# Block transposes into contiguous scratch with ScalarE reordering, and expert weight loads kept in program order, in a sparse-attention and expert-layer kernel

## The chip, the cores and the metric

The kernel runs on one core of a Trainium2 chip. Its metric is the device time of one execution in microseconds (us). Three runs of the kernel before took 335.82, 336.32 and 337.53 us; the median is 336.32 us. The engines are TensorE (PE, with its weight loads PEld), VectorE (DVE), ScalarE (ACT), GpSimd (POOL) and SyncE (SP), which here only issues DMAs.

## The reference

Attention over 4 batches of 8 heads, 768 positions, head dimension 64, followed by a layer of 8 experts to which every token is assigned once, each expert taking exactly 384 of the 3072 tokens:

```python
def _attn_ref(q, k, v, n_global, n_local):          # n_global 8, n_local 96
    scores = scale * np.matmul(q, k.transpose(0, 1, 3, 2))
    keep = is_global | is_local                      # first 8 keys, or the last 96 up to the query
    scores = np.where(keep, scores + bias[None], -1e9)   # bias: -slope(head) * distance
    a = np.exp(scores - np.max(scores, axis=-1, keepdims=True))
    a = a / (np.sum(a, axis=-1, keepdims=True) + 1e-09)
    return np.matmul(a, v)

def _moe_ref(x, w_gate, w1, w2):                     # x: (3072, 512), 8 experts, F 1024
    logits = x @ w_gate
    # tokens in order of falling logit take their expert while it has room (384 each)
    for e in range(E):
        h = np.maximum(x[assigned == e] @ w1[e], 0.0)
        out[assigned == e] = h @ w2[e]
```

## The kernel before

The program has three stages, one after the other: attention, routing, experts.

**Attention** runs over 8 units u; a unit is half a batch, four heads. Its order is written out by hand in the loop at L460, and every engine follows it. For a unit, q and k arrive as 128 x 24 x 64 tiles (`kr`, `qr`: partition = head and block of 24 positions). VectorE transposes 32 x 32 blocks of them (`blocks`, L265): two calls for k (`kT`), two for q (`qT`), each 128 x 768 elements, and it writes the result in natural order, that is with neighbouring elements 24 positions (96 bytes) apart. ScalarE then copies k into seven overlapping tiles of 8 + 120 keys (`kA_out`, L273). `scores` (L307) multiplies in three groups, `expo` (L321) exponentiates each group on ScalarE, `mask` (L328, L335) multiplies by the mask on VectorE.

While unit u does this, unit u-1, whose two head pairs are A and B, is finished: `av` (L355) multiplies by v, `oT_out` (L360, ScalarE) takes the product out of PSUM, `sums` (L386, L389) forms row sums and gate logits in the PSUM tile `pr`, `sums_out` takes them out on VectorE, beginning with the transpose `LT` (L399), and `tok` (L419) transposes the heads on TensorE into `pk`, which VectorE scales (L427). `pr` and `pk` share two PSUM buffers, so the second `tok` of A waits until `LT` has emptied `pr`. The keys and queries of unit u+1 are transposed in between: `kT` at the start of the unit, `qT(0)` before `LT` of A, `qT(1)` behind it. There is one `kr` and one `qr` buffer; the load of unit u+2 is issued by SP after the transposes of u+1.

**Routing** (L566 to L851) is a chain of small VectorE and TensorE steps, which ends with the row numbers `idi`.

**Experts** (L853): `gather` (L866) fetches the 384 tokens of an expert in three indirect DMAs issued by GpSimd, `load_x` transposes them (L878, L879), then follow 32 matmuls with w1 (L897), the relu (L900), 24 matmuls with w2 (L906), the copy (L909) and three indirect scatters (L910). The weights of experts 0 and 1 are loaded during attention. The twelve late ones (w1 and w2 of experts 2 to 7, `late_weights`, L548) go into memory that attention used, so they are issued by GpSimd after it. They, the gathers and the scatters are all DMAs of GpSimd's one queue (q0). In the text four calls of `late_weights` stand ahead of routing and two in each expert's pass, around `gather(e + 2)`; outside the hand-ordered stretches a scheduler may move them.

Of the kernel before, what the change touches and what calls it, by code (L numbers as in the profile page):

```python
# [9 lines left out]
FP32 = mybir.dt.float32  # L10
# [20 lines left out]
KT = 120  # L31
NT = 7
# [10 lines left out]
def kernel(  # L43
# [159 lines left out]
    with ExitStack() as actx:  # L203
# [21 lines left out]
                                channel_multiplier=-1)  # L225
        natp = actx.enter_context(tc.tile_pool(name="natp", bufs=1))
        ktp = actx.enter_context(tc.tile_pool(name="ktp", bufs=2))
        tp = actx.enter_context(tc.tile_pool(name="tp", bufs=3))
        ppa = actx.enter_context(tc.tile_pool(name="ppa", bufs=4))
        ppb = actx.enter_context(tc.tile_pool(name="ppb", bufs=5))  # L230
# [8 lines left out]
        NJ = S_ // 32  # L239
        qr = natp.tile([128, NJ, D_], FP32)  # L240
        kr = natp.tile([128, NJ, D_], FP32)
        kTn = natp.tile([128, 2, NT * KT], FP32)
        v7s = [natp.tile([128, 2, NT, D_], FP32, name=f"v7_{i}") for i in range(NB)]
        kAs = {}
        qTs = {}
        LASTK = S_ - KT * (NT - 1)

        def load_u(u, dst, src):
# [13 lines left out]
            nc.sync.dma_start(v7[8 : 8 + LASTK, :, NT - 1, :],  # L262
                              v[b, h : h + 2, KT * (NT - 1) : S_].rearrange("t u d -> u t d"))

        def blocks(dst, src, g):  # L265
            nc.vector.transpose(out=dst[:, g, 0:S_].rearrange("p (c j) -> p j c", j=NJ),  # L266
                                in_=src[:, :, 32 * g : 32 * g + 32])

        def kT(u):
            for g in range(2):  # L270
                blocks(kTn, kr, g)

        def kA_out(u):  # L273
            kA = ktp.tile([128, 2, NT, 128], FP32, tag="kA", name=f"kA{u}")
            kAs[u] = kA
            nc.scalar.copy(out=kA[:, :, :, 8:128], in_=kTn.rearrange("p g (i k) -> p g i k", i=NT))
            nc.scalar.copy(out=kA[:, :, :, 0:8],  # L277
                           in_=kTn[:, :, 0:8].rearrange("p g (o k) -> p g o k", o=1).to_broadcast([128, 2, NT, 8]))

        def qT(u, g):  # L280
            if g == 0:
                qTs[u] = ktp.tile([128, 2, S_], FP32, tag="qT", name=f"qT{u}")
            blocks(qTs[u], qr, g)

        wpieces = []
        for e in range(W_EARLY):
# [10 lines left out]
                nc.gpsimd.dma_start(dst, s_)  # L297

        def scores(u, g):
            kA, qTt = kAs[u], qTs[u]  # L300
# [141 lines left out]
        with tc.manual_schedule():  # L442
            load_u(0, kr, k)
            load_u(0, qr, q)
            nc.vector.memset(kTn[:, :, S_:], 0.0)
            for i in range(NB):
                nc.vector.memset(v7s[i][:, :, NT - 1, :], 0.0)
            kT(0)
            load_u(1, kr, k)
            qT(0, 0)  # L450
            qT(0, 1)
# [4 lines left out]
            kA_out(0)  # L456
            for t in range(2):
                nc.gpsimd.tensor_scalar(out=wgx[64 * t : 64 * t + 64, :, 8 * t : 8 * t + 8],
                                        in0=wg_sb[64 * t : 64 * t + 64], scalar1=LSCALE, scalar2=None, op0=ALU.mult)
            for u in range(NU + 1):  # L460
                A, Bp = 2 * (u - 1), 2 * (u - 1) + 1
                cur, prev, nxt = u < NU, u > 0, u + 1 < NU
                if cur:
                    ps = scores(u, 0)
                    expo(u, 0, ps)
                    if u == 0:
                        for h in range(4):
                            build_W(h)
                if nxt:
                    kT(u + 1)  # L470
                    if u + 2 < NU:
                        load_u(u + 2, kr, k)
                if cur:
                    mask(2 * u, 0)
                    mask(2 * u + 1, 0)
# [7 lines left out]
                if nxt:  # L483
                    qT(u + 1, 0)
                    kA_out(u + 1)
                if prev:
                    sums_out(A, pr)
                weight_piece()
                if cur:
                    ps = scores(u, 1)  # L490
                    expo(u, 1, ps)
                    if u == 0:
                        for h in range(4, 8):
                            build_W(h)
                if nxt:
                    qT(u + 1, 1)
                    if u + 2 < NU:
                        load_u(u + 2, qr, q)
                if cur:
                    mask(2 * u, 1)  # L500
                    mask(2 * u + 1, 1)
                if prev and cur:
                    for hf in range(2):
                        pk = tok(A, hf)
                        tok_out(A, hf, pk)
                if prev:
                    av(Bp)
                    oT_out(Bp, 0)
# [36 lines left out]
    def late_weights():  # L545
        if lates:
            dst, s_ = lates.pop(0)
            nc.gpsimd.dma_start(dst, s_)  # L548

    for _ in range(4):  # L550
        late_weights()
# [301 lines left out]
    def experts(first):  # L853
        with ExitStack() as fctx:
# [7 lines left out]
            def gather(e):  # L862
                for t in range(TSLAB):
                    s = TSLAB * e + t
                    xe = gp.tile([128, DM], BF16, tag="xe", name=f"xe_{s}")
                    nc.gpsimd.indirect_dma_start(  # L866
                        out=xe, out_offset=None, in_=x_tok[:, :],
                        in_offset=bass.IndirectOffsetOnAxis(ap=idi[:, s : s + 1], axis=0),
                    )
                    xes[s] = xe  # L870

            def load_x(e):
# [87 lines left out]
```

## Time and profile before

| | |
|---|---|
| profiled execution | 337.55 us |
| its span, first to last instruction | 335.7 us |
| mean granted TensorE clock | 0.933 of full |
| attention, up to the first late weight | 178.8 us |
| routing, to the first gather | 32.2 us |
| first gather to the first expert matmul | 21.3 us |
| experts, to the end of the span | 103.4 us |
| busy: PE, DVE, ACT, POOL | 268.1, 188.0, 108.3, 80.7 us |

A mean over the whole span says little here, since the three stages have different limits: VectorE is nearly always busy in attention and little later. So the stretches are read one by one. An engine follows its own order; where it stands idle, the trace gives the length and what released it in square brackets. The 1.85 us between the profiled execution's time and its span lie outside the instructions.

### The profile page before, as it was taken

Reading aid. Unit: us, or ns where it says so; the run is one execution under the profiler, and the core shown is the slowest. Engines: PE = TensorE matmul, PEld = TensorE weight load, DVE = VectorE, ACT = ScalarE, POOL = GpSimd, SP = SyncE. Lnnn points to the kernel's source line nnn. Section 1 sums busy time; section 2 is a strip of 40 time slices with the busy share of each in tenths; the row PEclk is TensorE's granted clock in tenths of the full one; section 3 lists DMA queues with packets and bytes.
Section 4 is the critical chain, followed back from the end, with each engine's and each line's share of the span. In section 5 each row is a group of like instructions: output and inputs, shape, how many; then the busy total and the mean of one; then the engine's idle time right before and its main releaser. Section 6 shows DMA issues by size and latency. Waiting matters only on the chain. (4 is left out here: it accounts for less than half of the span.)

```text
span 335.7 us, 7401 instructions
## 1 busy us (share of the span) xinstructions
PE 268.1 (80%) x3174; PEld 182.4 (54%) x3174; DVE 188.0 (56%) x300; ACT 108.3 (32%) x177; POOL 80.7 (24%) x126
## 2 busy tenths in 40 slices
PE   0479559896998979899997889505999989999950
PEld 0367448685876858688874443103555545555520
DVE  4984597999998897996724667102121421332220
ACT  1395044545352443634310010000442233234400
POOL 4050000002077000000006100524664644311330
PEclk9999959999997989999996999955999999999995
DMA  4599565658979965422025999996799333111220
GB/s 187 183 191 202 193 169 144 173 146 195 208 120 266 238 161 146 99 52 51 2 49 85 211 209 210 211 209 197 126 212 288 109 111 127 62 61 66 96 96 6
DMA packets 52569, 49.27 MB, mean 147 GB/s; under 512 B 29745, under 2 KB 44081, under 8 KB 52529
## 3 DMA queue, kind: packets, MB, share of 16 engines
q0 software_dynamic: 15680, 26.22, 37.5%
q1 hardware_dynamic: 36848, 22.50, 25.6%
q8 instruction: 27, 0.44, 0.6%
q14 instruction: 14, 0.11, 0.1%
HBM read 56.05 MB, written 9.44 MB: 195 GB/s over the span
## 5 line engine op out<-in xcount | busy, mean ns | idle before, releaser
L307 PE MATMUL ps<-qT,kA 32*128 32x215 f32 (+2 forms) x896 | 52.3, 368 | 15.4 <-DVE qT L266 11.4
L900 ACT ACTIVATE hT<-ph 128x384 bf16<-128x384 f32 x64 | 30.9, 490 | 87.0 <-PE ph L897 51.1
L307 PEld LDWEIGHTS ps<-qT,kA 32*128 32x128 f32 x896 | 43.7, 207 | 21.9 <-ACT kA L277 11.4
L321 ACT ACTIVATE P<-ps 128x860 f32<-128x860 f32 (+1 forms) x48 | 40.8, 887 | 39.6 <-PE ps L307 38.4
L355 PE MATMUL po<-P,v 128*64 128x215 f32 (+6 forms) x576 | 44.7, 312 | 0.0
L355 PEld LDWEIGHTS po<-P,v 128*64 128x64 f32 x576 | 37.4, 148 | 9.2 <-issue 3.4
L335 DVE TENSOR_TENSOR P<-P,Wm 128x860 f32<-128x860 f32 (+1 forms) x32 | 33.2, 1056 | 12.2 <-ACT P L321 11.0
L266 DVE STREAM_TRANSPOSE kTn<-kr 128x768 f32<-128x768 f32 x16 | 31.9, 2098 | 12.5 <-DMA kr<-in_k_dram 12.5
L879 DVE COPY xT<-pxe 128x512 bf16<-128x512 bf16 x24 | 9.5, 421 | 48.6 <-PE pxe L878 32.8
L909 DVE COPY ot<-po 128x512 f32<-128x512 f32 x24 | 16.6, 691 | 33.8 <-PE po L906 26.1
L866 POOL DMA_INDIRECT xe<-x_tok,idi x24 | 23.3, 972 | 46.2 <-DVE idi L720 21.3
L897 PE MATMUL ph<-xT,w_late 128*128 128x384 bf16 x192 | 32.7, 326 | 1.4 <-ACT hT L900 1.0
L419 PE MATMUL pk<-ident,oT 128*128 128x128 f32 x96 | 17.6, 295 | 19.9 <-DVE LT L399 18.3
L910 POOL DMA_INDIRECT out_dram<-ot,idi x24 | 23.5, 978 | 40.6 <-DVE ot L909 37.4
L906 PE MATMUL po<-w_late,hT 128*128 128x512 bf16 x144 | 32.9, 379 | 0.0
L266 DVE STREAM_TRANSPOSE qT<-qr 128x768 f32<-128x768 f32 x16 | 32.9, 2080 | 0.0
L906 PEld LDWEIGHTS <-hT 128*128 128x128 bf16 x192 | 18.2, 98 | 19.5
L548 POOL DMA_DIRECT2D w_late<-in_moe_w_dram x12 | 10.1, 865 | 74.6 <-DVE x L427 71.1
L386 PE MATMUL pr<-P,onesx 128*32 128x192 f32 (+11 forms) x768 | 27.6, 259 | 0.0
L897 PEld LDWEIGHTS <-w_late 128*128 128x128 bf16 x192 | 18.8, 98 | 14.9 <-issue 2.1
L360 ACT COPY oT<-po 128x384 f32<-128x384 f32 x32 | 15.4, 480 | 34.6 <-PE po L355 34.6
L386 PEld LDWEIGHTS pr<-P,onesx 128*32 128x32 f32 x768 | 24.6, 109 | 2.2
(137 smaller groups left out, 248.2 us busy)
## 6 DMA issues: line engine op xcount, KB each, us to landing
w_late<-in_moe_w_dram POOLq DMA_DIRECT2D x12, 1024.0 KB
kr<-in_k_dram SPq DMA_DIRECT2D x8, 768.0 KB
qr<-in_q_dram SPq DMA_DIRECT2D x8, 768.0 KB
v<-in_v_dram SPq DMA_DIRECT2D x32, 180.0 KB
w_early<-in_moe_w_dram POOLq DMA_DIRECT2D x8, 512.0 KB
x_tok<-x SPq DMA_DIRECT2D x32, 96.0 KB
v<-in_v_dram SPq DMA_DIRECT2D x32, 14.0 KB
v<-in_v_dram SPq DMA_DIRECT2D x16, 24.0 KB
```

Source lines behind the costliest of these rows:

```text
L266: nc.vector.transpose(out=dst[:, g, 0:S_].rearrange("p (c j) -> p j c", j=NJ), in_=src[:, :, 32 * g : 32 * g + 32])
L307: nc.tensor.matmul(ps[a // 2][:, a % 2, o : o + w], lhsT=kA[r, gd, i, :], rhs=qTt[r, gd, KT * i : KT * i + w], start=(gd == 0), stop=(gd = ...
L321: nc.scalar.activation(P[:, :, 0 : GW[g]], ps[w_][:, :, 0 : GW[g]], AF.Exp, scale=0.125)
L335: nc.vector.tensor_tensor(out=P[:, :, 0 : GW[g]], in0=P[:, :, 0 : GW[g]], in1=Wm[:, h0 : h0 + 2, lo : lo + GW[g]], op=ALU.mult)
L355: nc.tensor.matmul(po[n][bk][64 * t : 64 * t + 64, a - QB * bk : z - QB * bk], lhsT=v7[:, t, i, :], rhs=P[:, t, o + a - q0 : o + z - q0], ...
L386: nc.tensor.matmul(o_, lhsT=l_, rhs=r_, start=first[gq], stop=True, skip_group_check=True)
L419: nc.tensor.transpose(pk[:, bb, :], oTs[n][:, 3 * hf + bb].rearrange("c g r -> c (g r)"), ident)
L866: nc.gpsimd.indirect_dma_start(out=xe, out_offset=None, in_=x_tok[:, :], in_offset=bass.IndirectOffsetOnAxis(ap=idi[:, s : s + 1], axis=0),)
L897: nc.tensor.matmul(ph, lhsT=w1_of(e)[:, kc, 128 * fc : 128 * fc + 128], rhs=xT_e[:, kc, :, :].rearrange("p t n -> p (t n)"), start=(kc == ...
L900: nc.scalar.activation(hT[:, fc, :], ph, AF.Relu)
L906: nc.tensor.matmul(po, lhsT=hT[:, fc, 128 * t : 128 * t + 128], rhs=w2_of(e)[:, fc, :], start=(fc == 0), stop=(fc == NFC - 1))
L910: s = nc.gpsimd.indirect_dma_start(out=out[:, :], out_offset=bass.IndirectOffsetOnAxis(ap=idi[:, TSLAB * e + t : TSLAB * e + t + 1], axis= ...
```

## The change

VectorE now transposes into a scratch tile `tT` (two buffers, pool `ttp`) and writes it contiguously, with the 32 positions of a block side by side. ScalarE puts the elements in order: it reads the scratch with 128 bytes between neighbouring elements and writes natural order. For k there are three copies a half (720, 48 and 56 elements), for q one of 768. `kA` becomes two fixed tiles. In unit 0 the first masks now stand before `kT(1)`, and SP's loads for unit 1 stand, as before, behind the transposes that free their buffers. Last, the late weight loads and the gathers are marked to keep program order.

```diff
-        def blocks(dst, src, g):
-            nc.vector.transpose(out=dst[:, g, 0:S_].rearrange("p (c j) -> p j c", j=NJ),
-                                in_=src[:, :, 32 * g : 32 * g + 32])
+        def blocks(key, src, g):
+            t = ttp.tile([128, NJ, 32], FP32, tag="tT", name=f"tT_{key}_{g}")
+            nc.vector.transpose(out=t, in_=src[:, :, 32 * g : 32 * g + 32])
+            tTs[key, g] = t
...
+        def kA_out(u, g):
+            t = tTs.pop((f"k{u}", g)).rearrange("p j c -> p c j")
+            kA = kAs[u % 2][:, g]
+            n6 = NT - 1
+            nc.scalar.copy(out=kA[:, 0:n6, 8:128].rearrange("p i (c j) -> p i c j", j=NJ),
+                           in_=t[:, 0 : n6 * NC5, :].rearrange("p (i c) j -> p i c j", c=NC5))
+            nc.scalar.copy(out=kA[:, n6, 8 : 8 + LASTK].rearrange("p (c j) -> p c j", j=NJ),
+                           in_=t[:, n6 * NC5 : 32, :])
+            nc.scalar.copy(out=kA[:, :, 0:8],
+                           in_=t[:, 0:1, 0:8].to_broadcast([128, NT, 8]))
...
+        def qT_out(u, g):
             if g == 0:
                 qTs[u] = ktp.tile([128, 2, S_], FP32, tag="qT", name=f"qT{u}")
-            blocks(qTs[u], qr, g)
+            nc.scalar.copy(out=qTs[u][:, g, :].rearrange("p (c j) -> p c j", j=NJ),
+                           in_=tTs.pop((f"q{u}", g)).rearrange("p j c -> p c j"))
...
                 if nxt:
+                    for g in range(2):
+                        kA_out(u + 1, g)
                     qT(u + 1, 0)
-                    kA_out(u + 1)
+                    qT_out(u + 1, 0)
...
                 if nxt:
                     qT(u + 1, 1)
+                    qT_out(u + 1, 1)
...
-            nc.gpsimd.dma_start(dst, s_)
+            tc.keep_in_program_order(nc.gpsimd.dma_start(dst, s_))
...
-                    nc.gpsimd.indirect_dma_start(
+                    tc.keep_in_program_order(nc.gpsimd.indirect_dma_start(
```

On GpSimd, at the start of the experts, the queue before reads as follows (`w1_late` and `w2_late` are late weights, `xe_0` to `xe_2` the gathered tiles of expert 0).

```order
L548 DMA w1_late_2165<-in_moe_w1_dram 128x4x1024
L548 DMA w2_late_2166<-in_moe_w2_dram 128x8x512
L548 DMA w1_late_2165<-in_moe_w1_dram 128x4x1024
L548 DMA w2_late_2166<-in_moe_w2_dram 128x8x512
L548 DMA w1_late_2165<-in_moe_w1_dram 128x4x1024
L548 DMA w2_late_2166<-in_moe_w2_dram 128x8x512
L548 DMA w1_late_2165<-in_moe_w1_dram 128x4x1024
L548 DMA w2_late_2166<-in_moe_w2_dram 128x8x512
L548 DMA w1_late_2165<-in_moe_w1_dram 128x4x1024
L866 DMA xe_0_2570<-x_tok,idi_2183 128x512
L866 DMA xe_1_2572<-x_tok,idi_2183 128x512
L866 DMA xe_2_2574<-x_tok,idi_2183 128x512
```

In the changed program the same place, up to the first gather of expert 2 (`xe_6`):

```order
L576 DMA w1_late_2243<-in_moe_w1_dram 128x4x1024
L576 DMA w2_late_2244<-in_moe_w2_dram 128x8x512
L576 DMA w1_late_2243<-in_moe_w1_dram 128x4x1024
L576 DMA w2_late_2244<-in_moe_w2_dram 128x8x512
L894 DMA xe_0_2648<-x_tok,idi_2261 128x512
L894 DMA xe_1_2650<-x_tok,idi_2261 128x512
L894 DMA xe_2_2652<-x_tok,idi_2261 128x512
L894 DMA xe_3_2673<-x_tok,idi_2261 128x512
L894 DMA xe_4_2675<-x_tok,idi_2261 128x512
L894 DMA xe_5_2677<-x_tok,idi_2261 128x512
L576 DMA w1_late_2243<-in_moe_w1_dram 128x4x1024
L894 DMA xe_6_2680<-x_tok,idi_2261 128x512
```

Nine late weights stood ahead of the first gather, and now four do; the fifth stands behind the six gathers of experts 0 and 1, and the others follow two to a pass.

On ScalarE, in unit 2, between the two `oT` copies of pair A and the next exponentials, before:

```order
L360 COPY oT_581<-po_2_579 128x2x6x32
L360 COPY oT_581<-po_2_580 128x2x6x32
L276 COPY kA_638<-kTn 128x14x120
L277 COPY kA_638<-kTn 128x14x8
L321 ACTIVATE P_1_665<-ps_2_1_647 128x2x430
L321 ACTIVATE P_1_667<-ps_2_1_648 128x2x430
```

And in the changed program, up to the copy of the second half of q behind the exponentials:

```order
L370 COPY oT_615<-po_2_613 128x2x6x32
L370 COPY oT_615<-po_2_614 128x2x6x32
L279 COPY kA_164<-tT_k_0_606 128x6x120
L281 COPY kA_164<-tT_k_0_606 128x48
L283 COPY kA_164<-tT_k_0_606 128x7x8
L279 COPY kA_164<-tT_k_1_608 128x6x120
L281 COPY kA_164<-tT_k_1_608 128x48
L283 COPY kA_164<-tT_k_1_608 128x7x8
L292 COPY qT_678<-tT_q_0_676 128x768
L331 ACTIVATE P_1_704<-ps_2_1_686 128x2x430
L331 ACTIVATE P_1_706<-ps_2_1_687 128x2x430
L292 COPY qT_678<-tT_q_1_708 128x768
```

Two copies become seven ahead of the exponentials, and one more follows them. On VectorE the order in a unit stays as it was; only the form of the transposes changes.

## Rows read from the trace of the kernel before

**Rows 1.** By stretch: length, busy PE, PEld, DVE, ACT, POOL, granted clock, DMA share, GB/s.

```profile
72.80:91.87 19.07, 16.18 (x309) 13.38 (x308) 18.20 (x25) 8.59 (x12) 1.98 (x7) 1.00 0.79 176
...
149.94:165.89 15.95, 15.92 (x309) 13.38 (x308) 10.47 (x20) 6.92 (x10) 0.00 (x0) 1.00 0.11 28
...
230.04:326.00 95.96, 92.36 (x544) 50.46 (x544) 26.13 (x48) 30.93 (x64) 42.55 (x44) 0.97 0.45 122
```

**Rows 2.** Timeline of PE in units 1 to 3 (start, us, what, idle before).

```profile
45.82 0.90 PE L419 MATMUL pk<-ident,oT 128*128 128x128 f32 x3 [7.66 <-DVE LT L399]
...
55.02 1.74 PE L307 MATMUL ps<-qT,kA 32*128 32x215 f32 x32
...
74.46 2.52 PE L355 MATMUL po<-P,v 128*64 128x215 f32 x36
...
83.97 0.55 PE L419 MATMUL pk<-ident,oT 128*128 128x128 f32 x3 [2.85 <-DVE LT L399]
```

**Rows 3.** Timeline of DVE in unit 3.

```profile
75.91 3.99 DVE L266 STREAM_TRANSPOSE kTn<-kr 128x768 f32<-128x768 f32 x2
79.69 2.04 DVE L335 TENSOR_TENSOR P<-P,Wm 128x860 f32<-128x860 f32 x2
...
83.52 0.39 DVE L399 STREAM_TRANSPOSE LT<-pr 128x192 f32<-128x192 f32 x1
```

**Rows 4.** Timeline of ACT in unit 2.

```profile
62.89 1.67 ACT L321 ACTIVATE P<-ps 128x860 f32<-128x860 f32 x2 [0.24 <-PE ps L307]
66.88 0.48 ACT L360 COPY oT<-po 128x384 f32<-128x384 f32 x1 [2.32 <-PE po L355]
```

**Rows 5.** Groups by line and form on DVE and ACT (count, busy, mean ns).

```profile
L266 DVE STREAM_TRANSPOSE kTn<-kr 128x768 f32<-128x768 f32 x16 | 31.9, 2098 | 12.5 <-DMA kr<-in_k_dram 12.5
...
L412 DVE TENSOR_REDUCE Lb<-Gb 128x48 f32<-128x384 f32 x3 | 2.5, 844 | 0.1
...
L412 DVE TENSOR_REDUCE Lb<-Gb 128x16 f32<-128x128 f32 x1 | 0.4, 376 | 0.0
...
L276 ACT COPY kA<-kTn 128x1680 f32<-128x1680 f32 x8 | 12.7, 1593 | 23.0 <-DVE kTn L266 23.0
...
L277 ACT COPY kA<-kTn 128x112 f32<-128x112 f32 x8 | 2.2, 280 | 0.0
```

**Rows 6.** Timeline of the first units: SP's third load of k and its `kT`.

```profile
33.02 0.36 SPq L250 DMA_DIRECT2D kr<-in_k_dram  x1
...
37.76 3.99 DVE L266 STREAM_TRANSPOSE kTn<-kr 128x768 f32<-128x768 f32 x2 [8.27 <-DMA kr<-in_k_dram]
```

**Rows 7.** Timeline of POOL, last late weights and first gathers.

```profile
188.87 0.76 POOL L548 DMA_DIRECT2D w_late<-in_moe_w_dram  x1 [3.54 <-DMA w_late<-in_moe_w_dram]
210.96 1.08 POOL L866 DMA_INDIRECT xe<-x_tok,idi  x1 [21.33 <-DVE idi L720]
...
213.66 0.95 POOL L866 DMA_INDIRECT xe<-x_tok,idi  x1 [0.30 <-issue]
...
229.87 0.95 POOL L866 DMA_INDIRECT xe<-x_tok,idi  x1 [3.99 <-DMA w_late<-in_moe_w_dram]
...
274.41 0.99 POOL L866 DMA_INDIRECT xe<-x_tok,idi  x1 [3.76 <-PE pxe L878]
```

**Rows 8.** Timeline of PE at the first experts.

```profile
230.04 2.14 PE L878 MATMUL pxe<-ident_bf,xe 128*128 128x128 bf16 x16 [14.64 <-DMA xe<-x_tok,idi]
232.26 7.40 PE L897 MATMUL ph<-xT,w_early 128*128 128x384 bf16 x32
...
291.27 5.36 PE L897 MATMUL ph<-xT,w_late 128*128 128x384 bf16 x32
```

**Rows 9.** Busy time by stretch around the gathers, columns as in rows 1.

```profile
230.00:235.00 5.00, 4.79 (x25) 2.96 (x26) 1.70 (x4) 0.49 (x1) 3.78 (x5) 0.50 0.40 120
...
255.00:260.00 5.00, 5.00 (x31) 2.81 (x29) 0.36 (x1) 2.32 (x5) 2.93 (x3) 1.00 1.13 315
```

**Rows 10.** The same for the second behind a gather on an idle queue.

```profile
276.00:277.00 1.00, 1.00 (x6) 0.44 (x5) 0.63 (x1) 0.00 (x0) 0.69 (x2) 1.00 0.42 131
```

More of the change, by code (lines that the diff above doesn't have):

```diff
@@ L227 @@
         ktp = actx.enter_context(tc.tile_pool(name="ktp", bufs=2))
+        ttp = actx.enter_context(tc.tile_pool(name="ttp", bufs=2))
         tp = actx.enter_context(tc.tile_pool(name="tp", bufs=3))
@@ L241 @@
         kr = natp.tile([128, NJ, D_], FP32)
-        kTn = natp.tile([128, 2, NT * KT], FP32)
+        kAs = [natp.tile([128, 2, NT, 128], FP32, name=f"kA{i}") for i in range(2)]
+        NC5 = KT // NJ
         v7s = [natp.tile([128, 2, NT, D_], FP32, name=f"v7_{i}") for i in range(NB)]
-        kAs = {}
         qTs = {}
+        tTs = {}
         LASTK = S_ - KT * (NT - 1)
@@ L263, in load_v, with kT @@
                               v[b, h : h + 2, KT * (NT - 1) : S_].rearrange("t u d -> u t d"))
-        def blocks(dst, src, g):
-            nc.vector.transpose(out=dst[:, g, 0:S_].rearrange("p (c j) -> p j c", j=NJ),
-                                in_=src[:, :, 32 * g : 32 * g + 32])
[L269 to L278, printed above, removed]
+        def blocks(key, src, g):
+            t = ttp.tile([128, NJ, 32], FP32, tag="tT", name=f"tT_{key}_{g}")
+            nc.vector.transpose(out=t, in_=src[:, :, 32 * g : 32 * g + 32])
+            tTs[key, g] = t
+        def kT(u, g):
+            blocks(f"k{u}", kr, g)
+        def kA_out(u, g):
[8 more added lines that the diff above has]
+                           in_=t[:, 0:1, 0:8].to_broadcast([128, NT, 8]))
         def qT(u, g):
+            blocks(f"q{u}", qr, g)
+        def qT_out(u, g):
             if g == 0:
                 qTs[u] = ktp.tile([128, 2, S_], FP32, tag="qT", name=f"qT{u}")
-            blocks(qTs[u], qr, g)
+            nc.scalar.copy(out=qTs[u][:, g, :].rearrange("p (c j) -> p c j", j=NJ),
+                           in_=tTs.pop((f"q{u}", g)).rearrange("p j c -> p c j"))
         wpieces = []
@@ L299, in scores @@
         def scores(u, g):
-            kA, qTt = kAs[u], qTs[u]
+            kA, qTt = kAs[u % 2], qTs[u]
             ps = [ps_s.tile([128, 2, 512], FP32, tag=f"ps{w_}", name=f"ps{w_}_{u}_{g}") for w_ in range(2)]
@@ L444 @@
             load_u(0, qr, q)
-            nc.vector.memset(kTn[:, :, S_:], 0.0)
+            for i in range(2):
+                nc.vector.memset(kAs[i][:, :, NT - 1, 8 + LASTK : 128], 0.0)
             for i in range(NB):
                 nc.vector.memset(v7s[i][:, :, NT - 1, :], 0.0)
-            kT(0)
+            for g in range(2):
+                kT(0, g)
+                kA_out(0, g)
+            for g in range(2):
+                qT(0, g)
+                qT_out(0, g)
             load_u(1, kr, k)
-            qT(0, 0)
-            qT(0, 1)
             load_u(1, qr, q)
@@ L455 @@
                 load_v(n)
-            kA_out(0)
             for t in range(2):
@@ L468, with keys, first_masks @@
                             build_W(h)
[L469 to L475, printed above, removed]
+                def keys():
+                    if nxt:
+                        kT(u + 1, 0)
+                        kT(u + 1, 1)
+                        if u + 2 < NU:
+                            load_u(u + 2, kr, k)
+                def first_masks():
+                    if cur:
+                        mask(2 * u, 0)
+                        mask(2 * u + 1, 0)
+                if u == 0:
+                    first_masks()
+                    keys()
+                else:
+                    keys()
+                    first_masks()
                 if prev:
@@ L483 @@
                 if nxt:
+                    for g in range(2):
+                        kA_out(u + 1, g)
                     qT(u + 1, 0)
-                    kA_out(u + 1)
+                    qT_out(u + 1, 0)
                 if prev:
@@ L865, in gather @@
                     xe = gp.tile([128, DM], BF16, tag="xe", name=f"xe_{s}")
-                    nc.gpsimd.indirect_dma_start(
+                    tc.keep_in_program_order(nc.gpsimd.indirect_dma_start(
                         out=xe, out_offset=None, in_=x_tok[:, :],
                         in_offset=bass.IndirectOffsetOnAxis(ap=idi[:, s : s + 1], axis=0),
-                    )
+                    ))
                     xes[s] = xe
```

## Prediction

> **What bounds the kernel now.** I read first the busy times by stretch, since the three stages have different limits, and then each engine's timeline for what ended its waits. In attention a unit takes 19.07 us, VectorE is busy for 18.20 of them and TensorE for 16.18 [rows 1]. TensorE stands still once in a unit, at the second transpose of pair A: 2.85 us in unit 3, until VectorE's `LT` has emptied `pr` [rows 2]. VectorE comes to `LT` late because `kT` (3.99 us), the masks (2.04) and `qT(0)` (2.1) stand ahead of it [rows 3, 5]. What TensorE needs when nobody keeps it waiting is in the trace too: the last unit has no next keys to transpose and takes 15.95 us, 15.92 of them busy [rows 1]. That is the floor of a unit.
>
> The second place is the start of the experts. The row numbers are there at 210.96, when the first gather is issued, the third follows at 213.66, and yet TensorE waits 14.64 us for the gathered tokens, until 230.04 [rows 7, 8]. The last late weight ended at 229.87, which the wait of the eighth gather shows [rows 7]: the tokens came 0.17 us behind the nine weights that stood ahead of them in GpSimd's queue. From there TensorE is busy for 92.36 of 95.96 us [rows 1], so the experts are bound by matmuls, and an earlier start is an earlier end.
>
> **The transposes.** The 32 calls of 2.10 us each [rows 5] stay, with contiguous results. `LT` is a transpose that already writes contiguously, 0.39 us for 192 elements [rows 3]. Were all of that by the element, 768 would take 1.56 us; with 576 more at 1.19 ns, as the masks take (2.04 us for two of 860), 1.07; with 0.16 us less of a fixed part, 0.9. If the layout wasn't the reason, 2.1 stay. I take 1.0 in bounds of 0.9 and 2.1, since `LT` is the nearest row. Four calls a unit save 4.4 us, so VectorE's 18.20 falls to about 14: under the floor, and `LT` of pair A comes some 3 us earlier than now, which is more than the wait of 2.85 us.
>
> **The ScalarE copies** are the price. For a unit ScalarE moves 2 x 824 elements of k and 2 x 768 of q, 3184 in eight instructions, where it moved 1792 in two. Contiguous reading costs (1593 - 280) / (1680 - 112) = 0.84 ns an element [rows 5], and about 0.1 us an instruction. Reading at a step of 128 bytes isn't in the trace. The nearest row is VectorE's sum over heads, which reads at a step of 32 bytes: (844 - 376) / (384 - 128) = 1.83 ns an element; farther off is the strided write of the old transposes, about (2098 - 190) / 768 = 2.5 ns [rows 5]. So 0.84 to 2.5 ns, and I take 1.83.
>
> [...]
>
> Does ScalarE then set the unit? It follows its order, and there is a loop through it: the last `oT` copy of pair B, the gate matmuls, `LT` (0.39 us), a transpose (0.55), the next first scores (1.74), `av` (2.52), the second `oT` of A (0.48), seven copies, two exponentials (1.67), the copy of q's second half, two `oT` of B (0.96) [rows 2, 3, 4]. The times given make 8.3 us; the eight instructions add 0.8; the gate matmuls and some nine handovers of 0.06 (`LT` ends at 83.91, TensorE starts at 83.97) I put at 1.1; the elements add 3.184 us for each ns. The loop is 10.2 + 3.184 c: 12.9 us at 0.84, 16.0 at 1.83, 18.1 at 2.5. At my value it just meets the floor of 15.95, so I take 16.2 us a unit. `qT(0)` now also waits until ScalarE has emptied a scratch buffer, with `LT` queued behind it on VectorE; the first k copies end about 6.5 us into the unit, when VectorE has just done the masks, so that wait is under 0.5 us.
>
> Units 2 to 6 run from 55.02 [rows 2] to 149.94 [rows 1]: 94.92 us. Five at 16.2 make 81.0: **13.9 us gained** (4.4 at 2.5 ns, 15 at the floor).
>
> **Start-up.** Unit 1 waits for its third `kr`, which SP issues at 33.02 behind the v loads and which lands at 37.76; VectorE then stood idle for 8.27 us, and TensorE for 7.66 [rows 6, 2]. Those loads stand in SP's queue behind the second `kr`, which goes out when the first two transposes are over; short ones end 2.2 us earlier, and the row of loads moves with them, by some 2 us. Behind `kr`, three short transposes save another 3.3 us before `LT`, less about 1.5 for the wait on ScalarE's copies. I take 3.6 us. The eight copies ahead of the first scores and of `expo` in unit 0 cost up to 5 us there, but the wait for `kr` covers them; if that cover goes, the gain is 0. Bounds 0 to 5.
>
> **The late weights.** The first weight is landed at 188.87, since the ninth waits for its counter, the ninth at 229.87: 5.1 us each [rows 7]. Four end at about 204, before the gathers at 210.96. On an idle queue a gather issued at 274.41 moves its 131 KB by 277 [rows 7, 10], 2.6 us; the third tile issued at 213.66 is then there at 216.3. One tile's transposes and copy take 1.1 us, three took 2.2 (230.04 to 232.26) [rows 8], so the first expert matmul comes at 217.4 to 218.5; I take 218.0 for 232.26: 14.3 us. [...] **16.3 us gained.** Bounds: 12 (a gather lands as late as 5 us after issue, and the clock still falls) and 17.
>
> What it moves back: weights 5 to 12 now share the queue with gathers and scatters, two to a pass, each pair behind the scatters of the pass before. None is needed early: a pass takes about 11.5 us ((95.96 - 2.2 - 2.0) / 8), the last weight is issued early in the fourth, some 41 us after the first expert matmul, and needed in the middle of the eighth, at 86. The gathers behind them are nearer. In a pass the queue has two weights (10.2 us) and three gathers and three scatters of 131 and 262 KB, 3.7 us at the 315 GB/s that it moved in a busy stretch [rows 9]: 14 us for 11.5. It falls behind by some 2.5 us a pass, four passes long, and the gather of expert 5 lands some 50 us in, and is needed at 51. I count 1 us lost.
>
> **The sum.** 13.9 + 3.6 + 16.3 - 1.0 = 32.8 us. From the span of 335.70 that leaves 302.9, from the profiled 337.55 us 304.8. The median of the runs shown is 1.2 us below the profiled run, so against it 303.5.
>
> **The rivals.**
> A. ScalarE's strided reads cost as much as VectorE's strided writes. A unit takes 18.1 us, of 13.9 only 4.4 remain, and start-up loses some 1.5: 303.5 + 9.5 + 1.5 = 314.5. For it: the only other strides in the trace are slow. Against: the nearer row is a read.
> B. The queue of GpSimd falls behind more than I count. With 7 us for the gathers and scatters of a pass instead of 3.7, it is 13 us behind after four passes, the gather of expert 5 comes some 5 us late, and a scatter that holds its `ot` buffer adds a few: 6 to 9 us, about 311. For it: the weights alone fill 10.2 of 11.5 us. Against: at a DMA share of 1.13, with the last weights passing, TensorE was busy for 5.00 of 5 us [rows 9].
> C. The transposes stay at about 2 us whatever they write. Then attention gains nothing and loses some copies' time: about 321. `LT` speaks against it.
> D. Slower than before: ScalarE becomes the engine that sets attention. The six units 1 to 6 take 114.0 us now (35.9 to 149.94); to eat up the 16.3 us of the experts, a unit must take 21.7, and by the loop that is c = 3.6 ns an element. Above that the kernel loses; at 4.5 ns a unit takes 24.5 and the time is about 353. Nothing in the trace reads or writes so slowly, which is all against it.
>
> **How the numbers follow.** Forecast 0.62, with its own range 298 to 309 (the bounds of copies, start-up and gathers, each moving alone); A 0.17, B 0.13, C 0.04, D 0.04. Leaving out what lies above 317 and below 296 leaves out C, D and a little of each end, under 2 in 10. What a measurement of this kernel can tell from no change is about 0.5%, 1.7 us. Only D, and a mixture of A, B and C together, come near 336: faster 0.95, same 0.02, slower 0.03.
>
> **What would show it.** Right: transposes near 1.0 us, copies of 768 near 1.5 us, no wait of `tok` on `LT` above 0.5 us, the granted clock at full through units 4 and 5, the first expert matmul 7 to 8 us behind the first gather, no wait for `xe` later. Wrong: copies of q above 2 us and `expo` waiting behind them (A), TensorE waiting for `xe` in the passes of experts 4 and 5 (B), transposes at 2 us (C). The whole is wrong if the first gather's tokens still land more than 10 us after it.

## The result and the profile after

The changed kernel takes **302.09 us** (median of four, 300.85 to 304.7) where the kernel before took 336.92 in the same rounds: a ratio of 0.897, with a 95% interval of 0.890 to 0.905. A later timing on another chip gave 302.17 us and 0.896 (0.893 to 0.899). The profiled execution took 304.7 us, the longest of the four, 302.9 of them its span.

The busy times by stretch of the changed kernel come first: units 2 to 6 together, the last unit, and the experts up to the last scatter; columns as in [rows 1].

```profile
51.06:132.60 81.54, 81.38 (x1542) 68.56 (x1541) 67.95 (x108) 64.90 (x90) 14.67 (x32) 1.00 0.82 188
132.60:148.55 15.95, 15.92 (x309) 13.40 (x308) 10.47 (x20) 6.92 (x10) 0.00 (x0) 1.00 0.11 28
200.63:293.36 92.73, 89.56 (x530) 48.66 (x528) 24.77 (x45) 31.43 (x64) 47.91 (x50) 0.98 0.79 184
```

Five units took 94.92 us before; now they take 81.54, or 16.31 each, and TensorE is busy for all but 0.16 us of the whole. The last unit, which prepares no next keys, is as it was. In the experts look at the DMA share, 0.79 where it was 0.45: the weights pass there now.

Part of the gain of the five units is the granted clock. Here is the kernel before in unit 4 and from 104 to 106 us, behind TensorE's wait for `LT` of that unit (2.19 us, to 102.38), and then the changed kernel in unit 4:

```profile
91.87:111.89 20.02, 17.80 (x309) 14.54 (x308) 17.58 (x24) 8.60 (x12) 12.74 (x25) 0.91 0.95 209
104.00:106.00 2.00, 2.00 (x22) 1.73 (x20) 2.00 (x3) 0.48 (x1) 1.77 (x7) 0.50 1.15 227
```

```profile
83.58:99.89 16.31, 16.28 (x309) 13.69 (x308) 13.78 (x24) 13.00 (x18) 12.12 (x25) 1.00 1.02 228
```

In units 4 and 5 the granted clock fell to 0.50 behind that wait (from 104 to 106 and from 124 to 126 us), and TensorE was busy for 17.80 and 17.79 us with the matmuls that took 16.18 in unit 3: 3.2 us more in all. Behind the longer wait of unit 3, 2.85 us, it stayed at 1.00. In the changed kernel, without the waits, it is at 1.00 in all five units.

The groups by form, of the transposes and of the copies that feed `kA` and `qT`, answer to [rows 5]:

```profile
L269 DVE STREAM_TRANSPOSE tT_k<-kr 128x768 f32<-128x768 f32 x16 | 14.7, 954 | 4.6 <-DMA kr<-in_k_dram 4.6
...
L292 ACT COPY qT<-tT_q 128x768 f32<-128x768 f32 x16 | 24.8, 1556 | 0.0
L279 ACT COPY kA<-tT_k 128x720 f32<-128x720 f32 x16 | 23.7, 1484 | 6.3 <-DVE tT_k L269 6.3
...
L281 ACT COPY kA<-tT_k 128x48 f32<-128x48 f32 x16 | 4.4, 275 | 0.0
```

A transpose of the same 768 elements went from 2.10 to 0.95 us, only by writing contiguously. The three ScalarE forms read at a step of 128 bytes; the largest and the smallest make (1556 - 275) / (768 - 48) = 1.78 ns an element.

TensorE in unit 3, in order of time, where [rows 2] had its wait of 2.85 us:

```profile
75.08 0.93 PE L429 MATMUL pk<-ident,oT 128*128 128x128 f32 x6
75.93 2.52 PE L365 MATMUL po<-P,v 128*64 128x215 f32 x36
78.38 2.23 PE L317 MATMUL ps<-qT,kA 32*128 32x215 f32 x48
```

The six transposes to tokens now run in one piece behind the scores and `av` follows at once. The scores of the third group take 2.23 us where they took 1.96, though no wait is shown. With a copy more on ScalarE (x3 below) they take 2.72 and wait for `expo`, with its small copies moved away (x7) they take 1.96 again: they run at ScalarE's pace.

GpSimd's and TensorE's rows where the experts begin answer to [rows 7, 8]; first GpSimd:

```profile
161.46 3.27 POOL L576 DMA_DIRECT2D w_late<-in_moe_w_dram  x4 [62.61 <-DVE x L437]
192.91 1.08 POOL L894 DMA_INDIRECT xe<-x_tok,idi  x1 [28.18 <-DVE idi L748]
194.30 0.99 POOL L894 DMA_INDIRECT xe<-x_tok,idi  x1 [0.30 <-issue]
195.59 0.96 POOL L894 DMA_INDIRECT xe<-x_tok,idi  x1 [0.31 <-issue]
```

and TensorE, up to its first expert matmuls and at the pass of expert 4:

```profile
197.76 0.61 PE L906 MATMUL pxe<-ident_bf,xe 128*128 128x128 bf16 x8 [0.43 <-DVE fc L876]
198.66 0.38 PE L906 MATMUL pxe<-ident_bf,xe 128*128 128x128 bf16 x4 [0.29 <-DVE xT L907]
200.23 0.61 PE L906 MATMUL pxe<-ident_bf,xe 128*128 128x128 bf16 x4 [1.19 <-DMA xe<-x_tok,idi]
200.63 6.86 PE L925 MATMUL ph<-xT,w_early 128*128 128x384 bf16 x32
...
246.16 5.36 PE L925 MATMUL ph<-xT,w_late 128*128 128x384 bf16 x32
252.73 0.74 PE L906 MATMUL pxe<-ident_bf,xe 128*128 128x128 bf16 x8 [1.20 <-DMA xe<-x_tok,idi]
...
258.71 5.36 PE L925 MATMUL ph<-xT,w_late 128*128 128x384 bf16 x32
```

The third tile's wait is 1.19 us where the tokens were waited for 14.64 us, and the first expert matmul stands 7.72 us behind the first gather instead of 21.30. Two things are left: the first 32 matmuls took 6.86 us, not 5.36, and the pass of expert 4 lasts 12.55 us (246.16 to 258.71) where an undisturbed one takes 11.07, since expert 5's tokens came late.

With these rows the two spans can be set against each other from end to end (a pass is counted from its first w1 matmul to the next expert's):

| stretch | before | after | gain |
|---|---|---|---|
| to the first scores of unit 2 | 55.02 | 51.06 | 3.96 |
| units 2 to 6 | 94.92 | 81.54 | 13.38 |
| last unit, to the first late weight | 28.86 | 28.86 | 0 |
| routing, to the first gather | 32.16 | 31.45 | 0.71 |
| first gather to first expert matmul | 21.30 | 7.72 | 13.58 |
| pass of expert 0 | 12.86 | 12.32 | 0.54 |
| passes of experts 1 to 6 | 68.30 | 67.90 | 0.40 |
| the rest | 22.28 | 22.05 | 0.23 |
| span | 335.70 | 302.90 | 32.80 |

Not all of this need belong to the change. Routing's code is the same; in its first 9 us or so the granted clock was 0.65 before and 0.80 after. In a second profile of the changed kernel (x9 below) it was 1.00, and routing took 30.50 us.

### The profile page after: what moved, and what is told of

It is laid out like the page before. It is cut to its first block, busy times and chain, and to the rows that moved or that the text cites. A ratio compares the mean times of both kernels' runs of the same rounds, so it can differ in the third digit from the quotient of the medians.

```text
span 302.9 us, 7456 instructions
## 1 busy us (share of the span) xinstructions
PE 261.4 (86%) x3174; PEld 180.1 (59%) x3174; DVE 156.4 (52%) x301; ACT 143.8 (47%) x225; POOL 81.2 (27%) x126
## 5 line engine op out<-in xcount | busy, mean ns | idle before, releaser
L317 PE MATMUL ps<-qT,kA 32*128 32x215 f32 (+2 forms) x896 | 54.2, 369 | 20.6 <-ACT qT L292 11.6
L317 PEld LDWEIGHTS ps<-qT,kA 32*128 32x128 f32 x896 | 45.4, 207 | 27.2 <-ACT qT L292 12.2
L345 DVE TENSOR_TENSOR P<-P,Wm 128x860 f32<-128x860 f32 (+1 forms) x32 | 32.9, 1049 | 18.0 <-ACT P L331 10.5
L365 PE MATMUL po<-P,v 128*64 128x215 f32 (+6 forms) x576 | 40.4, 292 | 0.0
L365 PEld LDWEIGHTS po<-P,v 128*64 128x64 f32 x576 | 34.4, 136 | 7.6 <-issue 3.5
L576 POOL DMA_DIRECT2D w_late<-in_moe_w_dram x12 | 10.4, 874 | 69.1 <-DVE x L437 62.6
L279 ACT COPY kA<-tT_k 128x720 f32<-128x720 f32 x16 | 23.7, 1484 | 6.3 <-DVE tT_k L269 6.3
L292 ACT COPY qT<-tT_q 128x768 f32<-128x768 f32 x16 | 24.8, 1556 | 0.0
L617 PE MATMUL pw<-w_early,ident_bf 128*128 128x512 bf16 x51 | 19.8, 389 | 2.7 <-DVE x L437 0.6
L338 DVE TENSOR_TENSOR P<-P,Wm 128x860 f32<-128x860 f32 x16 | 16.3, 1064 | 10.2 <-ACT P L331 10.2
```

The source lines that it names most:

```text
L279: nc.scalar.copy(out=kA[:, 0:n6, 8:128].rearrange("p i (c j) -> p i c j", j=NJ), in_=t[:, 0 : n6 * NC5, :].rearrange("p (i c) j -> p i c j ...
L292: nc.scalar.copy(out=qTs[u][:, g, :].rearrange("p (c j) -> p c j", j=NJ), in_=tTs.pop((f"q{u}", g)).rearrange("p j c -> p c j"))
L345: nc.vector.tensor_tensor(out=P[:, :, 0 : GW[g]], in0=P[:, :, 0 : GW[g]], in1=Wm[:, h0 : h0 + 2, lo : lo + GW[g]], op=ALU.mult)
L365: nc.tensor.matmul(po[n][bk][64 * t : 64 * t + 64, a - QB * bk : z - QB * bk], lhsT=v7[:, t, i, :], rhs=P[:, t, o + a - q0 : o + z - q0], ...
```

## The experiments

Times are medians; each ratio is to the kernel before, timed on the same chip in the same rounds, with its 95% interval. Chips differ: the kernel before took from 336.9 to 339.2 us on those used here, so kernels of different calls are compared by ratio.

**x1, the order of late weights and gathers alone.**

```
+            tc.keep_in_program_order(nc.gpsimd.dma_start(dst, s_))          # late weights
+                    tc.keep_in_program_order(nc.gpsimd.indirect_dma_start(  # gathers
 (attention as in the kernel before)
```

> The kernel before with only the second part of the change: late weight loads and gathers stay in program order; attention is the old one. Theory (the two parts are separate and their gains add): between the first gather and the first expert matmul 7.7 us instead of 21.3, so 13.6 us, 0.5 more from the clock in the first 32 matmuls, and 1.2 to 1.5 back at the gather of expert 5: 12.6 us less than before, about 324. Rival (the parts help each other: the late weights also start earlier in the new kernel, and only that lets the gathers through): the four weights still end before the first gather at 211, so the rival has its gain in attention alone and gives here under 8 us, 329 or more.

Measured: 321.73 us, ratio 0.955 (0.949 to 0.961): 15.7 us less, 3 more than expected. TensorE in this kernel:

```profile
217.80 5.36 PE L897 MATMUL ph<-xT,w_early 128*128 128x384 bf16 x32 [0.18 <-DVE xT L879]
...
267.49 0.73 PE L878 MATMUL pxe<-ident_bf,xe 128*128 128x128 bf16 x8 [0.29 <-DMA xe<-x_tok,idi]
```

The first gather went out at 210.28, so 7.52 us behind it the experts began, as in the changed kernel: the order did this by itself. The profiled execution, 319.5 us, is the fastest of the four; in it the first 32 matmuls took 5.36 us, TensorE waited only 0.29 for the gather of expert 5, and routing took 30.49. These terms go beyond what was expected, but they differ between executions, so the 3 us are not shown to be the order's.

**x2, attention alone.** The two marks of x1 are taken out of the changed kernel.

> The changed kernel with the scheduler's own order of late weights and gathers, as before the change: nine weights ahead of the first third tile's use. Theory (gains add): the first late weight is issued at 161.5 as in the changed kernel, 17.3 us earlier than before, the ninth weight ends 51 us later at 212.5, the first expert matmul comes at about 215 for 232.3, the rest is as before: 17.3 us less, about 319.5. Rival (an earlier attention is given back by the queue, since the gathers still wait for the weights): under 8 us, 329 or more.

Measured: 317.63 us, ratio 0.942 (0.936 to 0.947): 19.8 us less. TensorE again:

```profile
212.50 2.13 PE L906 MATMUL pxe<-ident_bf,xe 128*128 128x128 bf16 x16 [16.22 <-DMA xe<-x_tok,idi]
214.72 7.21 PE L925 MATMUL ph<-xT,w_early 128*128 128x384 bf16 x32
```

The first expert matmul comes at 214.72, 17.54 earlier than in [rows 8] and where it was expected, behind a wait for the gathers of 16.22 us. The gain of attention isn't given back, and the wait isn't cured by it. Some 2 us of the gain lie behind that point: its passes 1 to 6 took 66.9 us, where those of the kernel before took 68.3, with stalls that come up again under x6. Together x1 and x2 gain 15.7 + 19.8 = 35.5 us, and the whole change 34.8: the parts add, within what such terms leave open.

**x3, one strided copy more, and x4, no strides.** In x3 ScalarE makes the first half of q twice; in x4 the copies read their scratch straight through, which leaves the reordering out.

```
x3             if g == 0 and u > 0:
+                nc.scalar.copy(out=junk.rearrange("p (c j) -> p c j", j=NJ),
+                               in_=t.rearrange("p j c -> p c j"))
x4 -            in_=tTs.pop((f"q{u}", g)).rearrange("p j c -> p c j"))
x4 +            in_=tTs.pop((f"q{u}", g)).rearrange("p j c -> p (j c)"))     # kA likewise
```

> The changed kernel, and each unit's first copy of q is made a second time into a buffer that nobody reads (768 elements read at a step of 128 bytes, 1.56 us on ScalarE in every unit from 0 to 6). Loop theory (ScalarE's order sets the unit of 16.3 us): nearly the whole 1.5 us comes through, a unit takes 17.6 to 17.9, six units and unit 0 make 9 to 10.5 us: about 312. Floor theory (TensorE's 15.95 us set the unit, and ScalarE has slack): under 0.5 us a unit, 302 to 305.

> The changed kernel with the ScalarE copies of k and q reading the scratch contiguously: the same eight instructions and sizes, but the reordering is left out, so the scores are of shuffled columns. Loop theory: at 0.84 ns an element a unit's copies take 3.0 us less, the unit falls to TensorE's floor of about 15.95 from 16.3 (1.8 us over five units), and unit 0 and 1, where ScalarE stands on the path, give 1 to 3 more: 297 to 300. Rival (the strides are no cost, or TensorE waits for something else than ScalarE): the copies stay near 1.5 us or the unit stays at 16.3, and the time at 302.

Measured: x3 312.82 us, ratio 0.927 (0.921 to 0.932); x4 297.80 us, ratio 0.881 (0.875 to 0.887). The first scores of units 2 to 4 on TensorE in x3:

```profile
53.99 1.74 PE L322 MATMUL ps<-qT,kA 32*128 32x215 f32 x32
...
66.01 2.72 PE L322 MATMUL ps<-qT,kA 32*128 32x215 f32 x48 [0.91 <-ACT P L336]
71.70 1.74 PE L322 MATMUL ps<-qT,kA 32*128 32x215 f32 x32
...
89.45 1.74 PE L322 MATMUL ps<-qT,kA 32*128 32x215 f32 x32
```

and in x4 the same, with ScalarE's copies by form below:

```profile
49.33 1.74 PE L316 MATMUL ps<-qT,kA 32*128 32x215 f32 x32
...
65.29 1.74 PE L316 MATMUL ps<-qT,kA 32*128 32x215 f32 x32
```

```profile
L291 ACT COPY qT<-tT_q 128x768 f32<-128x768 f32 x16 | 13.3, 832 | 4.3 <-DVE tT_q L269 3.9
L279 ACT COPY kA<-tT_k 128x720 f32<-128x720 f32 x16 | 12.7, 792 | 8.9 <-DVE tT_k L269 8.9
...
L281 ACT COPY kA<-tT_k 128x48 f32<-128x48 f32 x16 | 3.7, 229 | 0.0
```

With 1.56 us more on ScalarE a unit takes 17.7 us (71.70 - 53.99), 1.4 more than 16.31, and TensorE now waits 0.91 us in it for `expo`. With some 3 us less three of the five units take 15.96 to 16.01, the floor; the other two, with the DMA engines at a share of 0.99 and 1.03, take 16.27 and 16.43 without a wait that the profile shows. So the loop through ScalarE sets the unit, and the changed kernel stands just above the point where TensorE's own work takes over: at x3's slope the loop of the changed kernel is 17.7 - 1.56 = 16.2. The same copies cost (832 - 229) / (768 - 48) = 0.84 ns an element without the stride and 1.78 with it, a factor of 2.1.

**x5, TensorE kept busy before the first expert matmul.**

```
+                    if first and e == 0 and t < 2:
+                        for _ in range(2 + t):
+                            pf_ = ps_o.tile([128, DM], FP32, tag="po")
+                            nc.tensor.matmul(pf_, lhsT=ident_bf, rhs=w1_early[:, 0, 0, 0:512], start=True, stop=True)
```

> The changed kernel with five matmuls of 128x512 on TensorE whose result nobody reads, two behind the transposes of the first gathered tile and three behind those of the second, so that it hardly stands still between 197.3 and the first expert matmul. Theory (the clock falls there because TensorE is busy for only 1.39 of 3.30 us; it costs 1.5 us in the first 32 matmuls): they take 5.36 us in every profile instead of 6.86, the first of them comes no more than 0.4 later, and the time falls by about 1.2 us, to 301, with less spread. Rival (the clock's fall comes from elsewhere, or differs from run to run whatever TensorE does): the granted clock still shows 0.50 behind the first expert matmul, and the time stays or grows by the matmuls put in.

Measured: 304.09 us, ratio 0.896 (0.892 to 0.899), the changed kernel's own. In the profile the first 32 matmuls took 7.04 us and the granted clock was 0.62 and 0.60 in the two stretches from 200.6 to 205. TensorE also stood still for 1.28 us right ahead of them, released by nothing that the profile shows, and was busy for 1.58 of the 3.10 us before 200.6, so the edit didn't keep it busy as meant, and the theory is neither shown nor refuted. What bears on it is x9: the changed kernel, unaltered, in another execution. Its busy times by stretch, columns as above:

```profile
194.00:197.00 3.00, 2.29 (x9) 0.65 (x8) 0.46 (x2) 0.00 (x0) 2.33 (x3) 1.00 0.38 117
197.00:200.50 3.50, 2.11 (x23) 1.47 (x22) 1.78 (x6) 0.09 (x1) 2.76 (x3) 1.00 0.36 101
200.50:203.00 2.50, 2.50 (x17) 1.53 (x16) 0.00 (x0) 1.91 (x5) 1.94 (x2) 1.00 0.72 92
```

and of the changed kernel as first profiled:

```profile
194.00:197.70 3.70, 2.94 (x9) 0.75 (x8) 0.33 (x1) 0.00 (x0) 2.79 (x3) 1.00 0.34 99
197.70:200.60 2.90, 1.36 (x16) 1.10 (x16) 1.48 (x6) 0.00 (x0) 2.29 (x4) 0.94 0.36 107
200.60:203.60 3.00, 3.00 (x13) 1.48 (x11) 0.42 (x1) 0.66 (x2) 2.39 (x3) 0.50 0.69 99
```

The work ahead is nearly the same, and the granted clock falls to 0.50 in one execution and stays at 1.00 in the other. So the fall isn't fixed by the kernel. In the other profiles with this order the first 32 matmuls took 5.36 to 5.41 us in x1, x8 and x11 and 6.39 to 6.76 in x3, x4, x10 and x12, whose edits don't touch this place except in x11 and x12; what decides it stays open.

**x6, gathers ahead of both weights in a pass.**

```
-                if first:
-                    late_weights()
                 if e + 2 < N_EXP:
                     gather(e + 2)
                 if first:
+                    late_weights()
                     late_weights()
```

> The changed kernel, and in each pass the gathers of expert e + 2 stand ahead of both late weights instead of between them. Theory (the gather of expert 5 is 1.2 us late because it stands behind a weight of 5.1 us in GpSimd's queue): no wait for xe later than the first pass, pass of expert 4 takes 11.07 us instead of 12.55, and the time falls by 1.2 to 1.5, to 300.7. Rival (the queue as a whole is behind, whatever the order in a pass): the wait moves to another gather or to a weight, and the time stays at 302.

Measured: 304.64 us, ratio 0.899 (0.895 to 0.902): no gain. In the profile no gather is waited for behind the first pass, as the theory has it, but TensorE lost as much in short stalls, 0.77, 0.55 and 0.61 us in the pass of expert 0 and 0.89 later:

```profile
203.05 0.81 PE L924 MATMUL ph<-xT,w_early 128*128 128x384 bf16 x4 [0.77 <-issue]
204.41 0.81 PE L924 MATMUL ph<-xT,w_early 128*128 128x384 bf16 x4 [0.55 <-issue]
```

Two of them have no releaser in the profile; the other two are put down to the relu. The clock stayed at 1.00 there. The kernel before had such stalls too: its passes of experts 3 and 4 took 12.36 and 11.65 us instead of 11.07, 1.9 us in all. In time the rival holds; in the profile the pass of expert 4 did fall to 11.07, and that of expert 5, with the stall of 0.89, took 12.12. x11 and x12 below say more.

**x7, small copies of k on GpSimd, and x8, another start.**

```
x7 -            nc.scalar.copy(out=kA[:, n6, 8 : 8 + LASTK]...       # and kA[:, :, 0:8]
x7 +            nc.gpsimd.tensor_copy(out=kA[:, n6, 8 : 8 + LASTK]...
x8 -                if u == 0:
x8 -                    first_masks()
x8 -                    keys()
x8 +                keys()             # in unit 0 as in the others
x8 +                first_masks()      # and load_v(2), load_v(3) behind load_u(2, kr, k)
```

> The changed kernel with the four small copies of k a unit (48 and 56 elements, 0.28 and 0.29 us on ScalarE) made by GpSimd, which is idle there: ScalarE has 1.1 us less in a unit. Loop theory: the unit falls from 16.3 to the floor of 15.95 to 16.0, 1.6 us over five units, and unit 0 and 1 give up to 1 more: 299.5 to 300.5. Rival (GpSimd's copies are slow or come late, and the first scores then wait for kA): no gain, 302 or more.

> The changed kernel with its old order in unit 0 (transposes of the next keys ahead of the first masks) and the v loads of pairs 2 and 3 behind the third load of k in SP's queue instead of ahead of it. Theory (unit 0 is set by ScalarE, which stood idle 2.01 us before 21.47 for the transposes behind the masks; then by the third kr, which lands at 35.74): ScalarE's copies start at about 19.5, the third kr lands before 32, unit 2 starts about 2 us earlier than 51.06, and the time is near 300. Rival (the old order gives the 3.96 us of the start back, since VectorE then waits for the second kr with the masks behind it): unit 2 starts at 52 or later, 303 or more.

Measured: x7 298.16 us, ratio 0.881 (0.878 to 0.885); x8 300.23 us, ratio 0.886 (0.882 to 0.889). Against the changed kernel's 0.896 both gain, 1.7% and 1.2%. In x7 four of the five units take 15.96 to 15.99 us (49.80 to 65.77 for the first); unit 5, with a stall of 0.83 us on TensorE without a releaser, takes 17.00. Unit 2 starts at 49.80. GpSimd needs 0.53 and 0.48 us for copies that ScalarE makes in 0.28 and 0.29; only VectorE waits for them, 1.9 us in three waits. Attention gains 1.9 us up to the last unit (130.69 for 132.60). Another 2.3 lie at the very end, behind the last scatter:

```profile
286.76 0.97 POOL L938 DMA_INDIRECT out_dram<-ot,idi  x1 [0.76 <-DVEq L950]
```

The span ends 8.1 us after this scatter's start; in the changed kernel it ends 10.5 us after the last scatter's (292.39). The four versions with the copies on GpSimd (x7, x10 to x12) have 8.1 to 8.3, all the other profiles 10.4 to 10.7, before and after; why is open. So the loop theory has 1.9 us of x7's gain, not the whole.

In x8 ScalarE's copies start at 19.14 instead of 21.47, the third load of k goes out at 17.46 and its transposes at 32.26 wait for nothing, and unit 2 starts at 49.69, 1.4 us earlier than 51.06. The old order in unit 0 gives nothing back. The other 2 us of its gain aren't shown to be the edit's: in its profile, whose mean granted clock is 0.99, routing took 30.46 us and the first 32 matmuls 5.41.

**x9 to x12, together on one chip:** the changed kernel again; x7 and x8 in one; that with the gathers first, as in x6; and that with six late weights instead of four ahead of the first gather (`range(6)`).

> The changed kernel itself, timed on the same chip as the three versions beside it, so that differences of 1% can be read. Both theories: its ratio to the kernel before is 0.897 within 0.008, as it was first measured.

> The changed kernel with the small copies of k on GpSimd, the old order in unit 0 and the v loads of pairs 2 and 3 behind the third load of k. Theory (two different limits, the loop through ScalarE in units 2 to 6 and the order of unit 0, so the gains mostly add): units of 15.96 us from 16.3 (1.7 us), unit 2 starts near 48.5 for 51.06 (2.5 us): 4 us under the changed kernel on the same chip, ratio to it 0.987. Rival (both shorten the same stretch of unit 0 and 1): no more than the better of the two alone, 2.5 us under the changed kernel.

> The version with the small copies on GpSimd and the other start, and in each pass the gathers of expert e + 2 ahead of both late weights. Theory (the late gather of expert 5 costs 1.2 to 1.5 us): that much less than the same version without it. Rival (the executions differ by as much through short stalls of TensorE in the first passes, which the profile puts down to nothing): no difference over 0.5 us.

> The version with the small copies on GpSimd and the other start, and six late weights instead of four ahead of the first gather. Theory (at 5.1 us each six end 31 us after the first is issued, just as the first gather goes out 31.5 us after it, and two fewer are left for the passes, so the gather of expert 5 isn't late): 1 to 1.5 us less than the same version with four. Rival (the sixth weight still passes when the gathers are issued, and the first expert matmul comes up to 5 us later): slower by 1 to 5 us.

| | us | lowest, highest | ratio to before | interval |
|---|---|---|---|---|
| x9 changed kernel | 302.17 | 301.35, 305.88 | 0.896 | 0.893 to 0.899 |
| x10 both | 297.97 | 293.70, 298.10 | 0.881 | 0.877 to 0.885 |
| x11 gathers first | 295.29 | 292.90, 296.17 | 0.874 | 0.871 to 0.877 |
| x12 six ahead | 295.04 | 293.63, 297.04 | 0.875 | 0.872 to 0.878 |

x10 is 4.2 us under x9, the number expected, but its ratio is that of x7 alone, so by time the rival (no more than the better of the two) isn't excluded. The rows say that the two add in attention: unit 2 starts at 48.60 (49.80 and 49.69 in x7 and x8), and the last unit 3.6 us earlier than in x9. With the 2.1 us at the very end that makes 5.6; in this execution routing took 1.1 us more than in x9, and the first 32 matmuls 1.2 more (6.57 us for 5.36).

x12, 7.1 us or 2.4% under the changed kernel, and x11 beat both kernels of this case. Their intervals touch that of x10, so the step from x10 is likely but its size, 2.7 to 2.9 us, is not settled. In the profiles much of it isn't the edit: x12's unit 2 starts 1.0 us earlier by the same code, and x11's first 32 matmuls take 5.36 us where x10's took 6.57. The late gather's part can be read there: TensorE waited for expert 5's tokens in the pass of expert 4 in x9 (0.83 us) and x10 (0.71), as in the changed kernel. In x12 it waits for none behind the first pass, and each pass from the second on takes 11.07 us (240.83 to 251.90 for that of expert 4, which took 12.06 in x10): 1.0 us. With the gathers first (x11) the wait is at expert 6 instead, 0.45 us. So the queue is behind, a little, in the middle passes; six weights ahead of the gathers take that away, and their last one didn't hold the gathers up: TensorE waits 0.38 us for the second tile and 0.20 for the third.

## Why the prediction was right

The mechanisms came out, and the time with them: 302.09 us for 303.5. That the span agrees to 0.1 us (302.9) is luck. It is that of the slowest of four executions, x9's of the same kernel is 299.8, and in it five terms were off, by up to 1.5 us, and were made up by 2.8 us that the sum didn't have (routing, stalls and the last stretch).

- **Transposes.** 1.0 us forecast, 0.95 and 0.98 measured. The layout of the result was the reason: the shapes, the source and the order of the calls stayed. C is out.
- **ScalarE's copies.** 1.83 ns an element was taken from VectorE's strided reduction, 1.78 measured; A's 2.5 is out, and D's 3.6 further still. The choice of the nearest row, a read, over the strided write decided some 10 us. That it came so near is in part luck: the row is another engine's, a sum, at a step of 32 bytes and not 128, and no run varies the step.
- **The unit.** 16.2 forecast, 16.31 measured; 13.9 us for five, 13.4 measured. The loop stands: x3 pays for a copy, x4 gains only down to 15.96. What was named as the cost of the wait for `LT` was the wait itself; 3.2 us more of the old units were the clock behind it, which the sum has only inside the 94.92 us. The clock is at full through units 4 and 5 now, as the signs have it. The loop's constant of 10.2 was a little low: x3's 16.2 less 3.184 x 1.78 is 10.5. `qT(0)` and `qT(1)` do wait for ScalarE's `kA` copies, 7.8 us in nine times, the longest 1.9 in unit 1 and up to 0.99 in units 2 to 6, more than the 0.5 forecast, but the six transposes beside `LT` still ran in one piece.
- **Start-up.** 3.6 forecast, 3.96 measured. The cover by the third `kr` did go nearly: VectorE waited 1.08 us for it instead of 8.27, and x8, which takes the rest of that wait away, gains by ScalarE's earlier start in unit 0.
- **Late weights and gathers.** 14.3 forecast, 13.6 measured by the stretch from first gather to first expert matmul, and 0.7 from a routing that ran at a higher clock in its first part (0.80 for 0.65), which the sum didn't have.
- **The clock behind the gathers.** This is a term that was mis-sized: 2.0 forecast from the shorter wait (7.40 us, with a clock of 0.50 at first, less 5.36 at 1.00 [rows 8, 9]), 0.5 in the profiled execution, since the clock fell there all the same, to 0.50 behind 1.19 us of waiting. x9 and x1 have the whole of it, so 2.0 is what an execution without the fall gives. The same 2.0 stands in the 11.5 us that the prediction counts for a pass; an undisturbed one took 11.07. That the fall varies from execution to execution I hadn't seen, with one profile to read.
- **The gather of expert 5.** 1.0 forecast, 1.5 measured (12.55 for 11.07), at the place named; in x9 1.1. The sign "no wait for `xe` later" failed (1.20 us), though the sum had counted with such a wait. B, more than that, didn't come: a scatter did hold its `ot` buffer, 5.7 us on VectorE in two waits, and TensorE shows no wait for it.
- **Stalls of the kernel before** in its passes of experts 3 and 4 weren't in the sum. They are gone in the profiled execution of the changed kernel, 1.9 us, and this makes up for the clock and the gather. x9 and x1 don't have them either, x6 has others; with one profile of the kernel before it isn't shown whether they belong to it or to that execution. For the sum it was luck.

## What to carry to other kernels

Ask of a slow transpose or copy which side of it is strided, and where the stride can go: VectorE lost 1.1 us a call to a strided result, ScalarE pays 0.7 us for the same elements as a strided read, and had the time to spare until its own loop met TensorE's. A wait of the busiest engine can cost more than its length: look at the granted clock behind it (here 0.50 behind two waits of 2.19 and 2.44 us, which cost 3.2 us more). A loop through an engine is priced by following its order once around the unit, waits and handovers included, not by its busy share (ScalarE was busy for 80% of a unit when it began to set it). And what stands ahead in a shared DMA queue is a wait like any other (here 14.64 us with nine weights ahead of the tokens, 1.19 with four): place large loads by when they are needed, and count what they move back.

## What the runs showed of the hardware that was not expected

- The granted clock behind a short gap of TensorE differs between executions of one kernel: at 0.50 for some 3 us in one profile, at 1.00 in another, 1.5 us apart in the first 32 matmuls (6.86 and 5.36). In attention of the kernel before it fell behind waits of 2.19 and 2.44 us and not behind one of 2.85; in x1, with the same attention, it did fall behind the one of 2.85 (0.84 over that unit, which took 21.74 us for 19.07).
- TensorE shows stalls that the profile puts down to nothing: 0.35 us in the kernel before, 1.28 in x5, 0.77 and 0.55 in x6, 0.83 in attention of x7; others of 0.42 to 0.89 it puts down to the relu. With them profiles differ by 1 to 2 us. Their cause is open.
- A strided read of fp32 on ScalarE costs 1.78 ns an element, a contiguous one 0.84, measured in the same place of two kernels that differ only there. At 24.83 and at 30.31 us of the changed kernel 768 strided elements took 1.50 us each; the mean of all 16 copies is 1.56.
- GpSimd needs 0.53 us for a strided copy of 48 elements and 0.48 for one of 56, where ScalarE needs 0.28 and 0.29: the larger one is the shorter, so little of it goes by the element.
- The stretch from the last scatter's start to the end of the span is 8.1 to 8.3 us in the four versions with those copies on GpSimd and 10.4 to 10.7 in all others.
